# Agent attention with a feed-forward product on one core: units 2 and 3 take half of their second products in seven products per block, batches 2 and 3 get their maxima through DRAM, and the opening runs in another order

## The chip, the core and the metric

The kernel runs on one core of a Trainium2 chip. Its engines are named as in the profile: PE (TensorE, matmuls), PEld (the loading of weights into PE), DVE (VectorE), ACT (ScalarE), POOL (GpSimd) and SP (SyncE, which issues most transfers). The metric is the device time of one execution in microseconds (us). Time before: median 655.76 us of 3 runs (655.13 to 657.58).

## The reference

Eight batches of agent attention with 8 heads, 576 tokens, head size 64 and 32 memories. The tokens (4608 x 512) then go through w_in (512 x 2048), h - tanh(h), and w_out (2048 x 512):

```python
def _attn_ref(q, k, v, phi):
    a = np.exp(phi - np.max(phi, axis=2, keepdims=True))
    a = a / (np.sum(a, axis=2, keepdims=True) + 1e-09)
    k_m = np.einsum('bhsm,bhsd->bhmd', a, k)
    v_m = np.einsum('bhsm,bhsd->bhmd', a, v)
    scores = (1.0 / np.sqrt(q.shape[-1])) * np.matmul(q, k_m.transpose(0, 1, 3, 2))
    attn = np.exp(scores - np.max(scores, axis=-1, keepdims=True))
    attn = attn / (np.sum(attn, axis=-1, keepdims=True) + 1e-09)
    return np.matmul(attn, v_m)
...
h = x @ w_in
g = h - np.tanh(h)
return g @ w_out
```

## The kernel before

**Precision and products.** Large products run in fp16 pairs (high and low part), three matmuls for one. The weights arrive as 64-bit numbers, in blocks of 128 x 512 (512 KB); `conv` (words T) makes fp32 of a pair of blocks by three passes on DVE (L398, L403, L408) and the fp16 high part on ACT (L420). The low part is made in one of three ways: on DVE (`low`, Lv, L433), on ACT and POOL (`low_pool`, L, L449 and L452), or by PE and ACT (`low_pe`, Lp, L441, L442 and L444).

**Attention of a batch b.** X takes the maxima of phi over the tokens. Batches 0 and 1 use them in rows (L204, L209, then XT turns the result on PE, L218 and L220). For batches 2 and 3, XP spreads a diagonal over the partitions by an fp32 matmul (L170), and Y subtracts the result on DVE (L175, L181) ahead of the exponential on ACT. From batch 4 on, X writes the maxima to DRAM, XL loads them back to all partitions (`ms`), YM subtracts on POOL (L191, L197), and YE is the exponential. V (L238, L246) multiplies with k and v, N (L251 to L254) normalizes, U turns (L275), UV makes the fp16 pair of v (L517), S makes the scores (L290) and transposes them on DVE (L299). AM, AE, AD, AT and AS are the soft-max of a half (L318 to L338, L534); a v behind the name puts its POOL step on DVE.

**Products with the weights.** Since v_m has only 32 rows in a head, w_in is multiplied with v first: P (L543, L556) gives one of four blocks of 512 columns, PL its low part on DVE (L561), PLp the low part by PE and ACT (L568, L570).

**Units.** The tokens are cut into 18 units of 256; each has 4 blocks of 512 columns of the inner size. H (`mm1`, L591) is the first product of a unit and block; a or ap the cubic for h - tanh(h) on DVE and ACT (L606, L611, L616, L622); c or cv the low part of g on POOL or DVE (L627). M is the second product. `mm2` (L670) runs it as 24 matmuls of 512 columns. `mm2_blocks` (L727, L734), used from unit 4 on, treats the corrections as 2 x 2 blocks by seven products in place of eight: 8 matmuls of 512 columns and 28 of 256. It needs sums of blocks of g on DVE (F, `a_forms`, L640) and of w_out (G, `b_form`, L652), and collects part of its results in a PSUM tile x, which `evict` puts together at the end of a unit (L772, L773, L787 to L799). Units 0 to 3 are summed in two halves: OP saves the first half to DRAM, R loads it back, O adds the second half and writes the output (`save`, L697).

**Order.** Every engine runs its instructions in program order. Until the second block of unit 4 this order is the string START: each word starts a step, and its next occurrence runs the step's next part; words such as `i6:kv3` load blocks of weights into the buffers of the named tag, and Z is two matmuls without use (L808). Behind START a loop over the remaining blocks (slots from 18 on) runs with the plans PLAN and PLAN3.

Of the kernel before, what the change touches and what calls it, by code (L numbers as in the profile page):

```python
# [63 lines left out]
START = """
i0:gg i1:gg T00 T00 Z00 Z00 FX0 T00 X0 T00 YX0 Z00 Z00 Z00 Z00 Z00 Z00 Z00 Z00 Z00 Z00 i6:kv3 T03 i4:kv2 T03 i2:gg Z00
T02 T03 i3:gg T02 T02 Z00 KA0 Z00 Z00 Z00 KB0 Lp00 Lp00 o2:gg o3:gg Q00 T01 T03 XT0 Lp03 XT0 V00 Z00 Z00 T01 T01 T02
Q01 T01 o4:gg Lv01 o5:pp2 V01 N0 Z00 U0 L02 U0 Z00 S00 Z00 S01 T09 T09 T09 S00 o6:gg KA1 L02 KB1 AM00 S01 AM00 Lp03 UV0
UV0 o7:gg AM01 W0 T09 AM01 AE00 AE01 AD00 AD01 AD00 AT00 AD01 Z00 Z00 Z00 P00 AT01 FX1 P00 Lp09 PLp00 Z00 ASv00 P01
PLp00 ASv00 T10 Lp09 P01 AS01 H00 H00 T10 T11 PL01 i10:kv3 o9:pp4 X1 Q10 ap00 Q11 o1:gg AS01 T10 o0:pp2 T11 YX1 ap00
H10 XT1 T11 ap00 H10 XT1 T10 Lv10 ap00 c00 V10 V11 T11 L11 H11 N1 a10 U1 T08 i8:kv2 T08 UV1 U1 S10 UV1 T08 KA2 a10 T08  # L70
H11 a10 S10 H01 Lv08 a10 c10 S11 M00 ap11 AM10 W1 P10 H01 o10:pp5 o8:gg ap11 S11 ap11 M10 AM10 AE10 AM11 KB2 FA2 P10
Q20 AD10 L11 AM11 ap01 PL10 Q21 P11 T12 T12 ap01 AE11 ap11 AD10 T12 cv11 T12 P11 M11 AT10 AD11 AS10 AS10 ap01 H20 PL11
AD11 Lv12 AT11 T05 T05 ap01 T05 H21 OP1 cv01 H20 FX2 T05 ap20 H21 AS11 ap20 o11:gg AS11 X2 ap20 M01 a21 H31 L05 OP0 T04
T04 T04 a21 ap20 cv20 XP2 a21 H31 ap31 Y2 T04 L05 i14:kv3 L04 a21 L04 H30 c21 H30 a30 T13 M20 Y2 P02 i12:kv2 M21 T13
ap31 a30 P02 T13 V20 V21 a30 PL02 ap31 H02 H12 T06 T06 T06 T13 L13 OP2 T06 P12 a30 Lv06 ap31 T07 T07 N2 T07 cv30 T07 W2
M30 Lv07 P12 o12:kv2 cv31 H02 PL12 a02 P03 H12 P03 a02 T14 T14 T14 PL03 M31 ap12 a02 FA3 T14 OP3 L13 U2 ap12 Lv14 U2
UV2 o14:kv3 UV2 a02 H13 S20 ap12 S20 H13 ap12 H03 c02 AM20 a13 H03 T15 a03 P13 M02 P13 a13 S21 PL13 c12 AM20 H22 T15
a03 H23 a13 AE20 a13 G00 c13 S21 P20 AMv21 H22 AD20 a22 T15 T15 AD20 a03 a03 a22 G01 Lv15 AT20 P20 H23 a22 AMv21 AE21
cv03 ap23 R1 a22 ASv20 PL20 M12 ap23 M13 P21 ap23 FQ3 H32 ap23 P21 H32 ASv20 O1 O1 AD21 PL21 a32 H40 H40 G10 ap40 c22
R0 AD21 cv23 G20 AT21 ap40 a32 G11 ap40 H41 M03 H33 P22 AS21 H33 a32 a32 M22 P22 c32 O0 M23 X3 G21 H41 ap41 G30 ap33  # L80
G31 PL22 ap41 O0 ap33 ap40 KR30 R2 P23 P23 O2 ap41 c40 AS21 O2 ap33 ap33 F40 cv33 ap41 M32 M33 R3 O3 O3 PL23 c41
"""
# [273 lines left out]
def split_path(ctx, tc, c, ins, out):  # L356
    nc = tc.nc
# [332 lines left out]
    def save(u):  # L690

        sc = 1.0 / (S_G * S_W)
        ots = acc["r", u] if u in parts else [big.tile([P, DM], F32, tag="pr", name=f"ot{u}{tt}") for tt in range(2)]
        for tt in range(2):
            o = acc[u][tt]
            if u in parts:
                nc.vector.scalar_tensor_tensor(ots[tt], o, sc, ots[tt], op0=ALU.mult, op1=ALU.add)  # L697
            else:
                nc.scalar.activation(ots[tt], o, AF.Copy, scale=sc)
# [4 lines left out]

    def mm2_blocks(u, fb, first, last):
# [72 lines left out]
        acc["evict"] = (u, ra, rb)

    def evict():  # L780
        if "evict" not in acc:
# [5 lines left out]
        nc.vector.scalar_tensor_tensor(ra[:, 0], x[:, 1, lo], sc, ra[:, 1], op0=ALU.mult, op1=ALU.add)  # L787
        nc.vector.scalar_tensor_tensor(rb[:, 0], x[:, 1, hi], sc, ra[:, 0], op0=ALU.mult, op1=ALU.add)
        nc.vector.tensor_tensor(ra[:, 2], ra[:, 0], rb[:, 2], op=ALU.add)
        for th, r in ((0, ra[:, 1:3]), (1, rb[:, 0:2])):  # L790
            if th == (u == NUNIT - 1):
                nc.vector.tensor_tensor(rb[:, 1], rb[:, 0], rb[:, 2], op=ALU.add)
            r = r.rearrange("p a x -> p (a x)")
# [379 lines left out]
```

## Time and profile before

| | us |
|---|---|
| median of 3 runs | 655.76 |
| profiled execution | 655.77 |
| its span | 654.0 |
| PE busy | 639.2 (98%) |
| DVE busy | 518.8 (79%) |
| ACT busy | 375.0 (57%) |
| POOL busy | 251.4 (38%) |

The span is the time from the first to the last instruction of the profile; 1.77 us of the execution lie around it. Busy time of an engine is a sum over stages with different limits. PE's ends are modelled, so the durations of neighbouring matmuls overlap and the distance of their starts is the better price. A single late piece in the opening is seen better in the order of its instructions than in the shares.

### The profile page before, as it was taken

The numbers are of one execution on the slowest core, as the hardware profiler recorded it, in microseconds if no ns is written. First come the engines' busy times: TensorE is split into PE (matmuls) and PEld (weight loads), VectorE is DVE, ScalarE is ACT, GpSimd is POOL, SyncE is SP. The second block draws the span as 40 slices with busy tenths as digits, with TensorE's granted clock in tenths as the row PEclk, the third lists the DMA queues.
The fourth block names the chain that finished last, engine by engine and source line by source line (L and its number), as shares of the span: only waits on it lengthen the run. The fifth ranks groups of instructions, "written<-read, shape, count | busy, mean of one in ns | idle before, by whom it ended". The sixth has DMA issues, their size and how long they took to land.

```text
span 654.0 us, 15595 instructions
## 1 busy us (share of the span) xinstructions
PE 639.2 (98%) x6682; PEld 455.3 (70%) x6682; DVE 518.8 (79%) x786; ACT 375.0 (57%) x505; POOL 251.4 (38%) x173
## 2 busy tenths in 40 slices
PE   8889999999999999999999999999999999999996
PEld 4355656556557768777777677877687777887885
DVE  5889999999956687876897779777978686867773
ACT  3577686666524456554655566546655577666541
POOL 0225241232132154452536353624453455455531
PEclk9899999999999999999999999999999999999999
DMA  8999354402423302144323512532354333234201
GB/s 341 362 383 386 101 193 157 126 20 66 146 97 103 134 33 74 36 152 170 99 47 148 169 45 95 155 134 70 107 154 135 101 107 121 62 111 138 81 34 37
DMA packets 27724, 85.51 MB, mean 131 GB/s; under 512 B 3584, under 2 KB 4096, under 8 KB 26880
## 3 DMA queue, kind: packets, MB, share of 16 engines
q1 hardware_dynamic: 26352, 82.08, 36.9%
q10 hardware_dynamic: 1296, 2.36, 1.0%
q8 instruction: 54, 0.88, 0.5%
q14 instruction: 22, 0.18, 0.1%
HBM read 72.89 MB, written 11.54 MB: 129 GB/s over the span
## 4 chain that ended last, share of the span: by engine, by line
PE 72%; DVE 15%; issue 4%; DMA 4%; ACT 3%; POOL 2%; DVEq 0%; ACTq 0%; POOLq 0%
PE hs L591 18%; PE x L734 12%; PE o L727 12%; PE o L734 9%; PE o L670 6%; PE h L591 4%; DMA raw<-in_w_out_dram 3%; PE o1h L670 3%; DVE f L640 3%; PE pp L543 3%; DVE h L616 2%; DVE h L606 2%; DVE ph L561 2%; PE warm L808 2%; DVE wt L403 1%
## 5 line engine op out<-in xcount | busy, mean ns | idle before, releaser
L627 POOL TENSOR_TENSOR g<-h,g 128x1024 f16<-128x1024 f32 x64 | 138.6, 2166 | 322.2 <-ACT g L622 228.9
L591 PEld LDWEIGHTS <-ph 128*128 128x128 f16 x2304 | 176.9, 98 | 20.1 <-issue 6.0
L591 PE MATMUL hs<-ah,ph 128*128 128x256 f16 (+3 forms) x1152 | 151.5, 246 | 0.0
L606 DVE SCALAR_TENSOR_TENSOR h<-hs,u 128x1024 f32<-128x1024 f32 x54 | 65.8, 1219 | 90.3 <-ACT u L598 90.3
L622 ACT ACTIVATE g<-h 128x1024 f16<-128x1024 f32 x72 | 75.9, 1055 | 93.9 <-DVE h L616 91.9
L591 PE MATMUL hs<-al,ph 128*128 128x256 f16 (+3 forms) x576 | 127.6, 246 | 0.0
L611 ACT ACTIVATE u<-u,beta 128x1024 f32<-128x1024 f32 x72 | 82.4, 1147 | 52.8 <-DVE h L606 51.7
L727 PE MATMUL o<-wout_hi,g 128*128 128x512 f16 x432 | 104.7, 379 | 0.0
L734 PEld LDWEIGHTS <-f 128*128 128x128 f16 x896 | 87.7, 98 | 10.1
L616 DVE SCALAR_TENSOR_TENSOR h<-u,h 128x1024 f32<-128x1024 f32 x72 | 87.4, 1216 | 0.8 <-ACT u L611 0.7
L598 ACT ACTIVATE u<-hs 128x1024 f32<-128x1024 f32 x54 | 55.1, 1020 | 49.2 <-PE hs L591 44.9
L734 PE MATMUL x<-bt,f 128*128 128x256 f16 x672 | 82.5, 273 | 0.0
L734 PEld LDWEIGHTS <-g 128*128 128x128 f16 x672 | 64.4, 98 | 25.8 <-issue 4.3
L727 PEld LDWEIGHTS <-g 128*128 128x128 f16 x432 | 40.5, 98 | 43.9 <-issue 8.1
L640 DVE TENSOR_TENSOR f<-g 128x512 f16<-128x512 f16 x112 | 67.6, 643 | 4.3 <-POOL g L627 3.4
L670 PEld LDWEIGHTS <-g 128*128 128x128 f16 x384 | 36.7, 98 | 46.6 <-issue 3.4
L670 PE MATMUL o<-wout_hi,g 128*128 128x512 f16 x192 | 58.8, 379 | 0.0
L591 PE MATMUL h<-ah,ph 128*128 128x256 f16 (+3 forms) x384 | 49.6, 246 | 0.1
L591 PE MATMUL h<-al,ph 128*128 128x256 f16 (+2 forms) x192 | 42.4, 246 | 0.2 <-POOL al L534 0.2
L561 DVE SCALAR_TENSOR_TENSOR ph<-pp,ph 128x1024 f16<-128x1024 f32 x31 | 37.6, 1215 | 1.4 <-ACT ph L556 1.4
L556 ACT ACTIVATE ph<-pp 128x1024 f16<-128x1024 f32 x32 | 32.6, 1018 | 7.9 <-PE pp L543 5.4
L670 PE MATMUL o<-wout_lo,g 128*128 128x512 f16 x96 | 36.4, 379 | 0.0
(145 smaller groups left out, 967.0 us busy)
## 6 DMA issues: line engine op xcount, KB each, us to landing
q<-in_qt_dram SPq DMA_DIRECT2D x16, 576.0 KB, 4.7
kv<-in_kva_dram SPq DMA_DIRECT2D x16, 516.0 KB, 6.9
chk<-in_w_in_dram SPq DMA_DIRECT2D x16, 512.0 KB, 5.4
chk<-in_w_out_dram SPq DMA_DIRECT2D x16, 512.0 KB, 3.4
out_dram<-r SPq DMA_DIRECT2D x27, 256.0 KB, 2.2
kv<-in_kva_dram SPq DMA_DIRECT2D x6, 1032.0 KB, 9.0
raws<-in_w_in_dram SPq DMA_DIRECT2D x12, 512.0 KB, 7.3
raw<-in_w_out_dram SPq DMA_DIRECT2D x12, 512.0 KB, 6.4
```

Of the source, the lines that this page charges most:

```text
L561: nc.vector.scalar_tensor_tensor(pl, pa, S_P / (S_V * S_W), ph, op0=ALU.mult, op1=ALU.subtract)
L591: nc.tensor.matmul(hp[:, k, tu : tu + w], px[:, g, cs], d[ax][:, g, ta : ta + w], start=(n == 0), stop=(n == 5),)
L598: nc.scalar.activation(uu, hp, AF.Square, scale=1.0 / (S_A * S_P))
L606: nc.vector.scalar_tensor_tensor(h3, hp, C2 * S_G / (S_A * S_P), uu, op0=ALU.mult, op1=ALU.mult)
L611: nc.scalar.activation(uu, uu, AF.Square, bias=c["beta"])
L616: nc.vector.scalar_tensor_tensor(h3, uu, CC, hp, op0=ALU.add, op1=ALU.mult)
L622: nc.scalar.activation(gg[:, 0], h3, AF.Copy)
L627: eng.tensor_tensor(gg[:, 1], h3, gg[:, 0], op=ALU.subtract)
L640: nc.vector.tensor_tensor(o, x, y, op=op)
L670: nc.tensor.matmul(o, gx[:, k, P * tt : P * tt + P], wx[:, 4 * fb + k, :], start=(first and k == 0 and wx is wout_hi and gx is gh), stop=( ...
L727: nc.tensor.matmul(o[th], gg[:, 0, k, P * th : P * th + P], wout_hi[:, 4 * fb + k, :], start=(first and k == 0), stop=False)
L734: nc.tensor.matmul(dst, a(1 - n, kk), b(n, kk), start=(new and kk == 0 and n == 0), stop=(end and kk == 1 and n == 1))
```

## The change

The second products M22, M23, M32 and M33 (units 2 and 3, blocks 2 and 3) go through `mm2_blocks`, with words F22, F23, F32 and F33 for their sums of g. The assembly of `evict` is split into `sums` (four sums on DVE) and the rest; `save_blocks` puts units 2 and 3 together: the sums, two additions of o on DVE, then one addition per half on POOL of the first half that came back from DRAM. Both PSUM buffers of the first products are taken for x and hs by the word XA inside START, in place of slot 18. Batches 2 and 3 go through DRAM as the later ones do. START is written anew: block pairs of w_in are loaded and converted in another order, Lp02 and PLp01 move work from DVE to PE and ACT, four lows of weights go from DVE to ACT and POOL and two the other way, two lows of g go from DVE to POOL, and three half soft-maxes use another engine. The number of words Z is the same, 26.

```diff
-        if b > 3 and self.dram:
+        if b > 1 and self.dram:
...
+        acc["r", u] = [big.tile([P, DM], F32, tag="pr" if u < 2 else "ot", name=f"pr{u}{i}") for i in range(2)]
...
+    def sums(u):
+        ra, rb = acc.pop(("evict", u))
+        x, sc = acc["x"], 1.0 / (S_G * S_W)
+        nc.vector.scalar_tensor_tensor(ra[:, 0], x[:, 1, 0:256], sc, ra[:, 1], op0=ALU.mult, op1=ALU.add)
+        nc.vector.scalar_tensor_tensor(rb[:, 0], x[:, 1, 256:512], sc, ra[:, 0], op0=ALU.mult, op1=ALU.add)
+        nc.vector.tensor_tensor(ra[:, 2], ra[:, 0], rb[:, 2], op=ALU.add)
+        nc.vector.tensor_tensor(rb[:, 1], rb[:, 0], rb[:, 2], op=ALU.add)
+        return [r.rearrange("p a x -> p (a x)") for r in (ra[:, 1:3], rb[:, 0:2])]
+
+    def save_blocks(u):
+        rs = sums(u)
+        for r, o in zip(rs, acc[u]):
+            nc.vector.scalar_tensor_tensor(r, o, 1.0 / (S_G * S_W), r, op0=ALU.mult, op1=ALU.add)
+        yield
+        for th, (r, p) in enumerate(zip(rs, acc["r", u])):
+            nc.gpsimd.tensor_tensor(p, p, r, op=ALU.add)
+            nc.sync.dma_start(out[u * UT + P * th : u * UT + P * th + P, :], p)
+
+    def open_x():
+        acc["x"] = ps_h.tile([P, 2, 512], F32, tag="h", name="x")
+        acc["hp"] = ps_h.tile([P, 4, UT], F32, tag="h", name="hs")
...
-        "M": lambda u, fb: mm2(u, fb, fb in (0, 2), fb in (1, 3)), "R": load_part, "OP": save_part, "O": save,
+        "M": lambda u, fb: mm2_blocks(u, fb, fb == 2, fb == 3) if u in (2, 3) and fb > 1 else mm2(u, fb, fb in (0, 2), fb in (1, 3)),
+        "R": load_part, "OP": save_part, "O": lambda u: save_blocks(u) if u > 1 else save(u), "XA": open_x,
...
-        (-6, "XP{0} Y{0} | V{0}0 KR{0}1 QT{0}0"), (-5, "| V{0}1 N{0}"), (-4, "U{0} UV{0} ; W{0} | S{0}0 QT{0}1"),
+        (-6, "YE{0} | V{0}0 KR{0}1 QT{0}0"), (-5, "| V{0}1 N{0}"), (-4, "U{0} UV{0} ; W{0} | S{0}0 QT{0}1"),
...
 START = """
-i0:gg i1:gg T00 T00 Z00 Z00 FX0 T00 X0 T00 YX0 Z00 Z00 Z00 Z00 Z00 Z00 Z00 Z00 Z00 Z00 i6:kv3 T03 i4:kv2 T03 i2:gg Z00
+Z00 i6:kv3 Z00 Z00 Z00 Z00 T03 Z00 T03 T03 Z00 FX0 T03 X0 i4:kv2 i0:pp2 T02 i2:gg i3:gg i1:gg T02 T02 YX0 T01 T01 Z00
```

Three places of the new order follow, as the instructions stand on an engine: a line of the source, the operation, what is written and read (the number is that of the tile). Lines of the changed kernel stand one higher up to the second products. First SP in the opening, from the second load of q to the maxima of batch 1 (`pt`, in_phx). Before:

```order
L139 DMA q_253<-in_qt_dram 128x1152
L385 DMA raw_257<-in_w_out_dram 128x512
L385 DMA raw_261<-in_w_out_dram 128x512
L385 DMA raw_335<-in_w_out_dram 128x512
L113 DMA kv_337<-in_kva_dram 128x2064
L121 DMA kt_339<-in_kvt_dram 128x516
L113 DMA kv_343<-in_kva_dram 128x2064
L385 DMA raw_354<-in_w_out_dram 128x512
L104 DMA pt_411<-in_phx_dram 128x1152
```

Changed:

```order
L140 DMA q_317<-in_qt_dram 128x1152
L114 DMA kv_346<-in_kva_dram 128x2064
L122 DMA kt_348<-in_kvt_dram 128x516
L393 DMA raws_350<-in_w_in_dram 128x512 x2
L386 DMA raw_353<-in_w_out_dram 128x512
L386 DMA raw_437<-in_w_out_dram 128x512
L386 DMA raw_439<-in_w_out_dram 128x512
L386 DMA raw_468<-in_w_out_dram 128x512
L386 DMA raw_519<-in_w_out_dram 128x512
L105 DMA pt_525<-in_phx_dram 128x1152
```

A pair of blocks of w_in and one more block of w_out have come ahead of `pt`, and one load of k and v has gone behind it.

Second DVE, on the way from the norm of batch 1 (`kvn`) to the transpose of its first scores (`sc`); `h` is the cubic, `wt` a block of weights in the making, `vl` the low part of v. Before:

```order
L254 TENSOR_TENSOR kvn_670<-pkv_597,kr_667 128x256
L606 SCALAR_TENSOR_TENSOR h_672<-h_544,u_585 128x1024
L398 TENSOR_SCALAR wt_679<-raw_537 128x512
L398 TENSOR_SCALAR wt_680<-raw_532 128x512
L403 SCALAR_TENSOR_TENSOR wt_679<-raw_537,wt_679 128x512
L403 SCALAR_TENSOR_TENSOR wt_680<-raw_532,wt_680 128x512
L517 SCALAR_TENSOR_TENSOR vl_689<-ptr_674,vh_688 128x128
L408 SCALAR_TENSOR_TENSOR wt_679<-raw_537,wt_679 128x512
L408 SCALAR_TENSOR_TENSOR wt_680<-raw_532,wt_680 128x512
L616 SCALAR_TENSOR_TENSOR h_672<-u_585,h_672 128x1024
L299 STREAM_TRANSPOSE sc_702<-psc_693 128x576
```

Changed:

```order
L255 TENSOR_TENSOR kvn_716<-pkv_619,kr_713 128x256
L617 SCALAR_TENSOR_TENSOR h_680<-u_587,h_680 128x1024
L617 SCALAR_TENSOR_TENSOR h_684<-u_614,h_684 128x1024
L399 TENSOR_SCALAR wt_784<-raw_666 128x512
L399 TENSOR_SCALAR wt_785<-raw_596 128x512
L518 SCALAR_TENSOR_TENSOR vl_727<-ptr_718,vh_726 128x128
L404 SCALAR_TENSOR_TENSOR wt_784<-raw_666,wt_784 128x512
L404 SCALAR_TENSOR_TENSOR wt_785<-raw_596,wt_785 128x512
L409 SCALAR_TENSOR_TENSOR wt_784<-raw_666,wt_784 128x512
L409 SCALAR_TENSOR_TENSOR wt_785<-raw_596,wt_785 128x512
L300 STREAM_TRANSPOSE sc_772<-psc_763 128x576
```

The cubics of two units stand together on both sides of the norm, and the conversion of one pair of blocks still lies between the norm and the transpose.

Third DVE at the end of START, where the sums of unit 0 are saved; `f` are the new forms, `pr` the half sums and `hs` the buffer of the first product. Before:

```order
L616 SCALAR_TENSOR_TENSOR h_2126<-u_2108,h_2059 128x1024
L616 SCALAR_TENSOR_TENSOR h_2057<-u_2045,h_2057 128x1024
L697 SCALAR_TENSOR_TENSOR pr_2114<-o_1719,pr_2114 128x512
L697 SCALAR_TENSOR_TENSOR pr_2115<-o_1720,pr_2115 128x512
L151 TENSOR_REDUCE mx_2312<-pt_2014 128x2
L157 TENSOR_TENSOR dg_2314<-ident,mx_2312 128x256
L652 TENSOR_TENSOR bt_2120<-wout_lo 128x2048
L606 SCALAR_TENSOR_TENSOR h_2128<-h_2128,u_2317 128x1024
```

Changed:

```order
L697 SCALAR_TENSOR_TENSOR pr_2142<-o_1808,pr_2142 128x512
L697 SCALAR_TENSOR_TENSOR pr_2143<-o_1809,pr_2143 128x512
L617 SCALAR_TENSOR_TENSOR h_2152<-u_2146,h_2039 128x1024
L641 TENSOR_TENSOR f_2155<-g_1967 128x2x256 x2
L641 TENSOR_TENSOR f_2155<-f_2155,g_1967 128x2x256
L641 TENSOR_TENSOR f_2155<-g_1967,f_2155 128x2x256
L607 SCALAR_TENSOR_TENSOR hs<-hs,u_2211 128x1024
L641 TENSOR_TENSOR f_2239<-g_2027 128x2x256 x2
L641 TENSOR_TENSOR f_2239<-f_2239,g_2027 128x2x256
L641 TENSOR_TENSOR f_2239<-g_2027,f_2239 128x2x256
```

Where the maxima and the sums of w_out stood, the forms of f22 and f23 now stand; the maxima and the sums of w_out come earlier.

More of the change, by code (lines that the diff above doesn't have):

```diff
@@ L64 @@
 START = """
-i0:gg i1:gg T00 T00 Z00 Z00 FX0 T00 X0 T00 YX0 Z00 Z00 Z00 Z00 Z00 Z00 Z00 Z00 Z00 Z00 i6:kv3 T03 i4:kv2 T03 i2:gg Z00
[L66 to L79, printed above, removed]
@@ L80 @@
-R0 AD21 cv23 G20 AT21 ap40 a32 G11 ap40 H41 M03 H33 P22 AS21 H33 a32 a32 M22 P22 c32 O0 M23 X3 G21 H41 ap41 G30 ap33
-G31 PL22 ap41 O0 ap33 ap40 KR30 R2 P23 P23 O2 ap41 c40 AS21 O2 ap33 ap33 F40 cv33 ap41 M32 M33 R3 O3 O3 PL23 c41
+Z00 i6:kv3 Z00 Z00 Z00 Z00 T03 Z00 T03 T03 Z00 FX0 T03 X0 i4:kv2 i0:pp2 T02 i2:gg i3:gg i1:gg T02 T02 YX0 T01 T01 Z00
+Z00 Z00 T01 Z00 Z00 T00 Lp03 T00 Z00 KA0 Z00 XT0 Lp03 T00 T02 XT0 T01 KB0 Lp02 Z00 Z00 Z00 Z00 Z00 Z00 V00 Z00 L01
+o2:gg Lp02 o3:pp4 Z00 V01 T00 N0 T09 Q00 T09 L01 Lp00 U0 T09 W0 Q01 U0 UV0 S00 S01 Lp00 UV0 S00 KA1 i10:kv3 o1:gg P01
@@ new lines @@
+AM00 AM00 Z00 S01 T09 Z00 Z00 AM01 Z00 P01 AE00 PLp01 AM01 AD00 AE01 AD00 AD01 AD01 o5:pp4 o4:pp2 P00 AT00 o6:gg PLp01
+AT01 ASv00 ASv00 Lp09 P00 PLp00 PLp00 Lp09 T10 T10 T10 o7:gg T11 FX1 AS01 H00 Q11 AS01 o0:pp4 H10 X1 T10 H00 YX1 KB1
+i8:kv2 o9:pp4 XT1 T11 Lv10 H10 XT1 V10 V11 T08 T08 o8:gg Q10 T08 T08 T11 L08 o11:pp5 a00 L08 a10 H11 a00 a10 N1 U1 a00
+a00 UV1 U1 KB2 W1 H01 a10 S10 S11 H11 T12 UV1 T12 T12 a10 S10 AM10 ap11 T12 T11 L12 c10 c00 M00 H01 P10 AM10 ap11 S11
+AM11 ap01 L11 AE10 AM11 ap11 FA2 AD10 AE11 KA2 L12 Q20 ADv11 o10:gg P10 ap11 PL10 M10 ap01 AD10 Q21 i14:kv3 AT10 P11
@@ new lines @@
+ap01 cv11 T05 T05 FX2 i12:kv2 T05 L11 M11 P11 ASv10 ASv10 T05 L05 ap01 ADv11 AT11 OP1 PL11 H20 T04 cv01 L05 AS11 H20
+ap20 ap20 H21 T04 T04 T04 Lv04 ap20 AS11 T13 M01 H21 OP0 H30 a21 T13 a21 H31 T13 H30 T13 ap20 a21 H31 Lv13 ap31 P02
+ap30 P02 c20 T06 ap31 ap31 a21 c21 M20 X2 ap30 M21 ap30 PL02 ap31 c31 ap30 XL2 P12 o12:kv2 YM2 T06 T06 T06 Lv06 T07 T07
+T07 H02 H12 cv30 OP2 P12 H02 T07 Lv07 M30 PL12 H12 ap12 a02 P03 M31 T14 T14 T14 P03 PL03 a02 o14:kv3 a02 T14 YE2 ap12
+a02 V20 Lv14 T15 V21 ap12 N2 H13 OP3 T15 T15 U2 G00 H03 H22 ap12 H13 T15 a13 UV2 W2 a13 U2 G01 UV2 c02 H03 P13 cv12 a13
@@ new lines @@
+ap03 G20 G10 L15 P13 a13 PL13 ap03 H22 M02 S20 c13 H23 ap03 a22 L15 ap03 S20 AM20 a22 a22 S21 AM20 S21 AM21 AM21 R1 H23
+G21 FA3 c03 FQ3 AE20 AD20 M12 X3 a22 ap23 ap23 M13 AE21 AD20 G11 H32 ap23 AT20 ap23 O1 G30 H32 R2 H33 KR30 P20 XL3 G31
+AS20 ap32 O1 M03 ap32 c22 AD21 ap32 P20 PL20 XA AS20 R0 H33 ap33 ap33 O0 ap33 AD21 F22 ap32 H40 c23 H40 P21 ap40 F23 O0
+ap40 cv32 P21 ap33 ap40 AT21 PL21 F32 c33 M22 M23 H41 F33 O2 ap40 H41 P22 ap41 ap41 O2 P22 M32 ap41 ap41 PL22 c40 M33
+F40 O3 P23 P23 YM3 R3 PL23 cv41 O3 ASv21 ASv21
@@ L675, in load_part @@
     def load_part(u):
-        acc["r", u] = [big.tile([P, DM], F32, tag="pr", name=f"pr{u}{i}") for i in range(2)]
+        acc["r", u] = [big.tile([P, DM], F32, tag="pr" if u < 2 else "ot", name=f"pr{u}{i}") for i in range(2)]
         for r, p in zip(acc["r", u], parts[u]):
@@ L692, in save @@
         sc = 1.0 / (S_G * S_W)
-        ots = acc["r", u] if u in parts else [big.tile([P, DM], F32, tag="pr", name=f"ot{u}{tt}") for tt in range(2)]
+        ots = acc["r", u]
         for tt in range(2):
             o = acc[u][tt]
[L696 to L699, printed above, removed]
+            nc.vector.scalar_tensor_tensor(ots[tt], o, sc, ots[tt], op0=ALU.mult, op1=ALU.add)
         yield
@@ L777, in mm2_blocks @@
                 prod(*m, end=m is ms[-1])
-        acc["evict"] = (u, ra, rb)
+        acc["evict", u] = (ra, rb)
+    def sums(u):
[17 more added lines that the diff above has]
+        acc["hp"] = ps_h.tile([P, 4, UT], F32, tag="h", name="hs")
     def evict():
-        if "evict" not in acc:
+        u = next((k[1] for k in acc if isinstance(k, tuple) and k[0] == "evict"), None)
+        if u is None:
             return
-        u, ra, rb = acc.pop("evict")
-        x, o, t0 = acc["x"], acc[u], u * UT
+        o, t0 = acc[u], u * UT
         sc = 1.0 / (S_G * S_W)
         lo, hi = slice(0, 256), slice(256, 512)
[L787 to L793, printed above, removed]
+        for th, r in enumerate(sums(u)):
             if u == NUNIT - 1 and th == 1:
@@ L915, in split_path @@
     for sl, (u, fb) in enumerate(slots, 18):
-        if sl == 18:
-            acc["x"] = ps_h.tile([P, 2, 512], F32, tag="h", name="x")
-            acc["hp"] = ps_h.tile([P, 4, UT], F32, tag="h", name="hs")
         todo = ["", "", ""]
```

## The prediction

> **What bounds the kernel now.** I read the windows first, because one average over the span mixes stages with different limits. A row gives the stretch, its length, then for each engine busy microseconds and instructions, then the granted clock, the share of DMA time and GB/s.
>
> ```profile
> core 0: us, PE busy (x) PEld busy (x) DVE busy (x) ACT busy (x) POOL busy (x), PEclk, DMA share, GB/s
> ...
> 20.00:40.00 20.00, 16.54 (x205) 7.01 (x203) 16.53 (x33) 11.94 (x21) 7.34 (x7) 0.91 0.97 363
> 40.00:60.00 20.00, 16.89 (x224) 12.58 (x223) 19.17 (x29) 15.65 (x26) 4.45 (x3) 1.00 1.00 379
> 60.00:180.00 120.00, 119.94 (x1144) 70.80 (x1142) 115.98 (x152) 77.33 (x99) 33.65 (x24) 1.00 0.37 128
> 180.00:200.00 20.00, 20.00 (x160) 11.40 (x158) 11.96 (x18) 4.53 (x6) 5.51 (x3) 1.00 0.23 79
> 200.00:640.00 440.00, 438.79 (x4784) 337.27 (x4783) 337.41 (x521) 255.98 (x342) 197.36 (x127) 1.00 0.33 105
> ```
>
> From 60 us PE is full to the end. The waits of PE from 60 to 640 us say the same: one line, 1.0 us in all.
>
> ```profile
> PE pp L543 <- DVE kvn L254: 1.0, 3, 0.4
> ```
>
> So the time is the moment at which PE becomes full (the first second product, M00, at 59.0) plus all the work that PE has from there. Two things move the end: an earlier or later M00, and less or more PE work behind it. A third can appear: DVE is busy 115.98 of 120 us from 60 to 180, so it follows PE with 4 us to spare, and if it falls behind, PE waits again.
>
> **Fewer columns in the second products.** Three steps of the chain that ended last price them: one block of the plain scheme, and the two parts of a block in the seven-product scheme (start, us, engine, what, line, count).
>
> ```profile
> 162.74 5.18 PE o L670 x24
> ...
> 604.64 1.73 PE o L727 x8
> ...
> 607.24 1.75 PE x L734 x16
> ```
>
> A plain block has 24 matmuls of 512 columns, 5.18 us (0.216 each). A block in the other scheme has 8 of these (1.73) and 28 of 256 columns, at 1.75 / 16 = 0.109 each 3.06: together 4.79. Blocks M22, M23, M32 and M33 change over: 4 x (5.18 - 4.79) = **-1.56**. All of it counts, since PE never waits there; it counts for nothing only if a new wait stands behind these blocks.
>
> **Maxima through DRAM.** Batches 2 and 3 lose the fp32 matmul of the diagonal (L170).
>
> ```profile
> 89.47 0.60 PE L170 MATMUL pmx<-dg,ones 128*128 128x256 f32 x2
> 89.90 0.27 PE L591 MATMUL h<-ah,ph 128*128 128x256 f16 x1
> ```
>
> The two rows start 0.43 apart, so the pair costs PE 0.43; twice, **-0.86**. What replaces it runs elsewhere: two transfers and a subtraction on POOL.
>
> ```profile
> mxd<-mx SPq DMA_DIRECT2D x4, 1.0 KB, 3.0
> ms<-mxd SPq DMA_DIRECT2D x4, 128.0 KB, 5.3
> L191 POOL TENSOR_TENSOR e<-e,ms 128x1024 f32<-128x1024 f32 x4 | 9.6, 2400 | 0.0
> ```
>
> 3.0 + 5.3 + 2.4, the two tail rows (1.2 together, half of L191 for less than a quarter of its elements) and the exponential at about 1.2 make some 13 us. In the new order X2 stands behind M20, and V20, the first matmul that needs the result, behind M31. Between them PE has M21, M30 and M31 (3 x 5.18 = 15.5) and two first products of 24 matmuls of 256 columns (2 x 2.6), 20.7. I take the way through DRAM as hidden, with some 8 us to spare, so at 0; if ms waits behind larger loads by more than that, PE stands at V20 and each further us is lost.
>
> **The opening.** Until M00 the transfers are busy 97 to 100% of the time, and PE has waits. The piece that sets M00 begins with X1, the maxima of batch 1, for which pt1 must land. Rows of SP, of DVE and of PE:
>
> ```profile
> 10.46 10.67 SPq L385 DMA_DIRECT2D raw<-in_w_out_dram  x2
> ...
> 36.32 0.33 SPq L104 DMA_DIRECT2D pt<-in_phx_dram  x1
> ```
>
> ```profile
> 42.36 1.33 DVE L204 TENSOR_REDUCE mx<-pt 128x2 f32<-128x1152 f32 x1
> 43.62 1.22 DVE L606 SCALAR_TENSOR_TENSOR h<-h,u 128x1024 f32<-128x1024 f32 x1
> 44.75 1.28 DVE L408 SCALAR_TENSOR_TENSOR wt<-raw,wt 128x512 uint32<-128x512 uint32 x2
> ...
> 48.35 1.21 DVE L616 SCALAR_TENSOR_TENSOR h<-u,h 128x1024 f32<-128x1024 f32 x1
> 49.49 1.28 DVE L433 SCALAR_TENSOR_TENSOR wout_lo<-wt,wout_hi 128x512 f16<-128x512 f32 x2
> 50.69 0.15 DVE L251 TENSOR_SCALAR kr<-pkv 128x2 f32<-128x2 f32 x1
> ...
> 51.41 1.22 DVE L606 SCALAR_TENSOR_TENSOR h<-h,u 128x1024 f32<-128x1024 f32 x1
> 52.76 0.76 DVE L398 TENSOR_SCALAR wt<-raw 128x512 uint32<-128x512 uint32 x2
> 53.44 1.28 DVE L403 SCALAR_TENSOR_TENSOR wt<-raw,wt 128x512 uint32<-128x512 uint32 x2
> 54.64 0.28 DVE L517 SCALAR_TENSOR_TENSOR vl<-ptr,vh 128x128 f16<-128x128 f32 x1
> 54.84 1.28 DVE L408 SCALAR_TENSOR_TENSOR wt<-raw,wt 128x512 uint32<-128x512 uint32 x2
> ...
> 57.17 0.78 DVE L299 STREAM_TRANSPOSE sc<-psc 128x576 f32<-128x576 f32 x1
> ```
>
> ```profile
> 58.36 0.71 PE L290 MATMUL psc<-q,kT 64*32 64x288 f32 x16
> 59.00 0.39 PE L670 MATMUL o<-wout_hi,g 128*128 128x512 f16 x1
> ```
>
> SP stood 10.67 us at one load of w_out that had no free buffer, and issued pt1 at 36.32; X1 ran 42.36 to 43.62. In the new order the loads up to and with pt1 are 17 blocks of weights of 512 KB, four of 576 KB (q and phi), three of 1032 KB and two of 258 KB (k and v; sizes from the shapes): 14,620 KB, 14.97 MB. At the 379 GB/s of the window they take 39.5 us, from 0.74 us on: pt1 lands at about 40.2, and X1 ends at 41.5, **2.1 earlier** than before. This holds if SP stands nowhere long, since the loads fill a queue; it is the weakest term.
>
> Behind X1 DVE then has, up to the transpose of S10 (starts one apart in the rows above): pairs of weight passes, 2 x 0.68 (L398) and 6 x 1.20 (L403, L408); one pair of L433, 1.20; two each of L606 (1.13) and L616 (1.14), 4.54; the norm, 0.72; vl, 0.20. That is 15.2. Before, the same stretch was 13.55 (43.62 to 57.17). So the transpose starts at 41.5 + 15.2 + 0.2 (the waits that were in it before) = 56.9, ends 0.7 later, S11 follows at once in the new order and takes 0.64 (58.36 to 59.00): M00 at 58.25, **-0.75**. Bounds: the whole 2.1 if DVE's rows fit into its waits as they move, and nothing if a load comes late.
>
> PE gets two more pieces ahead of M00: Lp02 (two fp32 matmuls of 512 columns and two fp16 ones) and PLp01, the three passes of a product again.
>
> ```profile
> 31.55 0.41 PE L543 MATMUL pp<-win_hi,vh 64*32 64x512 f16 x8
> ...
> 32.32 1.13 PE L441 MATMUL pw<-wt,idw 128*128 128x512 f32 x2
> 33.28 0.38 PE L442 MATMUL pw<-wout_hi,nid 128*128 128x512 f16 x1
> ```
>
> At most 2 x (1.13 + 0.38) and 3 x 0.41 with two of 0.38: 5 us at the outside. PE has 6.6 us without work from 20 to 60, so I cost them at nothing; half of that cover is ahead of X1, and without it 1 or 2 us of the lead would go.
>
> **The end of the opening, DVE and POOL.** Prices of what they gain and lose (busy, mean ns):
>
> ```profile
> L640 DVE TENSOR_TENSOR f<-g 128x512 f16<-128x512 f16 x112 | 67.6, 643 | 4.3 <-POOL g L627 3.4
> L640 DVE TENSOR_TENSOR f<-g,f 128x512 f16<-128x512 f16 x56 | 24.8, 442 | 1.9
> L787 DVE SCALAR_TENSOR_TENSOR r<-x,r 128x256 f32<-128x256 f32 x14 | 5.9, 418 | 2.1 <-ACT r L773 2.1
> L175 DVE TENSOR_TENSOR e<-e,pmx 128x1024 f32<-128x1024 f32 x2 | 2.4, 1218 | 0.0
> ```
>
> DVE gains four times the forms (2 x 0.643 + 2 x 0.44 = 2.2), two times four sums (4 x 0.42 = 1.7), and one soft-max row more (of the transpose's size, 0.8): 12.9. It loses two of L175 with diagonal and tails (2 x 2.4, the small ones taken as one more of its size), two lows of g (its size, 2 x 1.2), four of L433 (4 x 0.6) and one PL (1.2): 10.8. So **DVE has about 2 us more in all**, but the losses lie early and the gains late, before the third block of unit 4 at some 200 us. There the window 180:200 has DVE at 11.96 of 20: 8 us free, for a surplus of some 10 behind an early relief that gives it about as much lead. I cost it at 0. POOL gains two maxima with their tails (2 x 3.6), four additions (half of L191 each, 4.8), and two lows of g at 2.4 or less: some 17 us, where it was busy 33.65 of 120.
>
> [...] The row L640 f<-g has a mean of 643 ns, and the trace has single ones much longer:
>
> ```profile
> L640 DVE TENSOR_TENSOR f<-g x112: 382/419/1968, 184.7 to 643.1; 128x512 f16<-128x512 f16 x112
> ```
>
> [...]
>
> **Sum.** Against the profiled run of 655.77 (span 654.0), which stands 0.01 over the median of 655.76: -0.75 - 1.56 - 0.86 = -3.17, so **652.6**.
>
> **Rivals.**
> 1. The whole lead of X1 reaches M00 (2.1 in place of 0.75): 651.2. For it: every wait of PE in the opening hangs on DVE or ACT. Against: DVE has 1.65 us more to do behind X1.
> 2. The lead is lost, because a weight block comes late: T10 and T08 need blocks that wait for buffers of the products: 653.4, or 653.9 with half a us more.
> 3. PE has longer pauses in the opening and gets a slower clock. The window 20:40 has 0.91 granted, which costs 0.09 x 20 = 1.8. One more such stretch: 652.6 + 1.8 = 654.4. The order of the warm-up matmuls changes, their number doesn't, so I hold this for small. [...]
> 4. Slower: the forms at the end of the opening become the bound. Where POOL is at work, each of the two f<-g of a block takes 1.97 in place of 0.42, four blocks 4 x 2 x 1.55 = 12.4; less the some 5 us that DVE is ahead, PE waits 7.4: 660.0. It decides from the point at which DVE has less than 12 us of lead and free time at M22. Against: 8 free us in 180:200 and the early relief; POOL is not busy all the time.
> 5. The change does less than it says: the matmuls of 256 columns cost as much as those of 512, 112 x 0.107 = +12, 664.6. The chain's row of 16 in 1.75 excludes it nearly.
>
> **How the numbers follow.** A measurement of this kernel can tell some 0.5%, 3.3 us, from no change: faster is under 652.5, slower over 659.0. The forecast has 0.50, rival 1 0.15, rival 2 0.16, rival 3 0.09, rival 4 0.08, rival 5 0.02. The forecast lies just at the bound, so a little under half of it counts as faster: with rival 1, 0.38; slower is rivals 4 and 5, less the part of 4 that stays under 659: 0.08; the rest, 0.54, is no change. The range goes from 650.0 (rival 1 and 1.2 us of the 1.8 that the slow clock costs today) to 657.0 (rival 3 with half of the 5 us that the extra PE work could cost): 0.85 of the cases.
>
> **What would show it.** In the profile after: M00 at about 58.2, X1 ending at 41.5; no wait of PE over 1 us in sum from 60 to 200; the four blocks with 28 matmuls at 0.109 each; V20 and V30 without a wait on the exponential; forms of f22 to f33 with a mean under 0.8. It is wrong if X1 is not earlier than 43, if PE waits at M22 to M33 for f, or if the clock in the first 60 us is under 0.9 in more than one window.

## The result and the profile after

The changed kernel takes 658.99 us (median of 22 runs, 655.24 to 671.86) against 655.45 before (22 runs, 654.78 to 657.92): ratio 1.0054 (1.0041 to 1.0066). It is about 0.5% slower, where 652.6 was forecast. The run of 671.86 fell in a slower state of the chip (clock 0.949) and is not in the ratio. The profiled run took 658.27 (span 656.5, M00 at 60.21). The windows of the changed kernel, in the columns of before:

```profile
core 0: us, PE busy (x) PEld busy (x) DVE busy (x) ACT busy (x) POOL busy (x), PEclk, DMA share, GB/s
...
20.00:40.00 20.00, 16.13 (x238) 6.59 (x227) 14.24 (x30) 10.29 (x19) 7.46 (x6) 1.00 1.00 391
40.00:60.00 20.00, 17.06 (x234) 13.73 (x234) 19.71 (x34) 17.32 (x30) 5.39 (x4) 1.00 0.96 353
60.00:180.00 120.00, 116.49 (x1105) 70.14 (x1093) 114.51 (x147) 76.44 (x98) 50.80 (x31) 1.00 0.39 131
180.00:200.00 20.00, 20.00 (x245) 15.43 (x243) 18.19 (x30) 8.71 (x11) 10.66 (x9) 1.00 0.22 72
```

PE was full from 60 to 180 before (119.94) and is not now (116.49), while POOL went from 33.65 to 50.80. The waits of PE from 60 to 200 (total, times, longest):

```profile
PE psc L291 <- DVE ph L562: 1.5, 1, 1.5
PE pkv L239 <- ACT e L201: 0.9, 1, 0.9
PE h L592 <- DVE h L607: 0.7, 1, 0.7
PE h L592 <- DVE h L617: 0.4, 1, 0.4
```

That makes 3.5 us, all between 122 and 144, where before had none. M00 is 1.2 later, and behind it, with the waits taken off, 2.2 less is left (before: 654.0 - 59.0 - 1.0 of waits = 594.0; after: 656.5 - 60.2 - 4.5 = 591.8). So the profiled run comes out: 655.8 + 1.2 + 3.5 - 2.2 = 658.3. The 2.2 is what is left over in this sum, not a measurement of its own. The median is another 0.7 higher; that part is put down to the clock below, but no run isolates it.

The 1.2 is also that of one profile. Four kernels of the experiments have the same order up to M00 and, like this profile, no stretch of lower clock ahead of it: their M00 came at 59.62 to 59.91, so the new opening costs 0.6 to 1.2 against the 59.0 of before.

Where DVE is late ahead of two of these waits (those at 123 and 142), its rows and POOL's tell why. Which memory a row reads is taken from the tile's pool in kernel.py: PSUM where the pool says so, as for the products of PE, else SBUF. POOL, then DVE, at the subtraction of batch 2's maxima:

```profile
108.35 2.97 POOL L192 TENSOR_TENSOR e<-e,ms 128x1024 f32<-128x1024 f32 x1 [5.86 <-DMA ms<-mxd]
...
107.18 1.29 DVE L404 SCALAR_TENSOR_TENSOR wt<-raws,wt 128x512 uint32<-128x512 uint32 x2
108.39 3.49 DVE L409 SCALAR_TENSOR_TENSOR wt<-raws,wt 128x512 uint32<-128x512 uint32 x2
```

The second L409 row (from 108.99, 2.89 in place of 0.68) ended at 111.88, 0.56 after POOL's row. From there DVE ran late, and ACT behind it: the exponential for the wait at 123 stood behind a conversion that waited for DVE.

```profile
120.65 1.23 ACT L421 ACTIVATE wout_hi<-wt 128x512 f16<-128x512 f32 x2 [1.27 <-DVE wt L409]
121.79 1.15 ACT L201 ACTIVATE e<-e 128x1152 f32<-128x1152 f32 x1
```

And at a sum of w_out (G10):

```profile
137.78 2.42 POOL L628 TENSOR_TENSOR g<-h,g 128x1024 f16<-128x1024 f32 x1 [10.41 <-ACT g L623]
...
136.98 1.22 DVE L653 TENSOR_TENSOR bt<-wout_hi 128x2048 f16<-128x2048 f16 x1
138.12 3.16 DVE L653 TENSOR_TENSOR bt<-wout_hi,bt 128x2048 f16<-128x2048 f16 x1
141.20 1.21 DVE L562 SCALAR_TENSOR_TENSOR ph<-pp,ph 128x1024 f16<-128x1024 f32 x1
142.33 1.21 DVE L617 SCALAR_TENSOR_TENSOR h<-u,h 128x1024 f32<-128x1024 f32 x1
```

The sum of 1.2 us began after POOL's row, stood until that ended at 140.20, and ended 1.08 later. The two rows behind it read PSUM; beside POOL's next row (L453, from 140.15 on) they take their usual 1.21. In this profile DVE loses time beside POOL only in rows that read nothing but SBUF, such as these two (2.89 in place of 0.68, 3.16 in place of 1.22), and only to a POOL row that began first. Not every such row loses time; the last section says which. An estimate, from each stretched row against the usual length of the same row: from 60 to 200 DVE stood behind POOL for 8.9 us, where it was 3.0 in before. Before lost 2.0 of these between 125 and 145 without a wait of PE, so the loss alone does not make a wait: it has to fall ahead of a row that PE needs soon.

### The profile page after: what moved, and what is told of

The parts are those of the page before. It is cut to its first block, busy times and chain, and to the rows that moved or that the text cites. A ratio compares the mean times of both kernels' runs of the same rounds, so it can differ in the third digit from the quotient of the medians.

```text
span 656.5 us, 15803 instructions
## 1 busy us (share of the span) xinstructions
PE 638.0 (97%) x6758; PEld 460.7 (70%) x6758; DVE 523.8 (80%) x796; ACT 380.3 (58%) x513; POOL 275.9 (42%) x186
## 4 chain that ended last, share of the span: by engine, by line
PE 68%; DVE 18%; issue 6%; POOL 3%; DMA 2%; ACT 2%; ACTq 0%; SPq 0%; DVEq 0%; POOLq 0%
PE hs L592 19%; PE x L732 13%; PE o L725 13%; PE o L732 10%; PE o1h L671 3%; DVE f L641 3%; DVE h L617 3%; PE pp L544 3%; DVE h L607 2%; DVE wt L404 2%; DVE wt L409 2%; POOL g L628 2%; PE o L671 2%; DVE ph L562 2%; PE warm L825 1%
## 5 line engine op out<-in xcount | busy, mean ns | idle before, releaser
L628 POOL TENSOR_TENSOR g<-h,g 128x1024 f16<-128x1024 f32 x66 | 144.4, 2190 | 290.8 <-ACT g L623 186.1
L592 PE MATMUL hs<-ah,ph 128*128 128x256 f16 (+3 forms) x1216 | 157.2, 245 | 0.0
L592 PE MATMUL hs<-al,ph 128*128 128x256 f16 (+3 forms) x608 | 133.1, 245 | 0.0
L725 PE MATMUL o<-wout_hi,g 128*128 128x512 f16 x464 | 112.6, 379 | 0.0
L732 PEld LDWEIGHTS <-f 128*128 128x128 f16 x960 | 93.9, 98 | 10.9
L732 PE MATMUL x<-bt,f 128*128 128x256 f16 x720 | 88.4, 273 | 0.0
L641 DVE TENSOR_TENSOR f<-g 128x512 f16<-128x512 f16 x120 | 72.6, 645 | 4.3 <-POOL g L628 3.4
L592 PE MATMUL h<-ah,ph 128*128 128x256 f16 (+2 forms) x320 | 44.1, 251 | 2.1 <-ACT ph L571 0.9
L671 PE MATMUL o<-wout_hi,g 128*128 128x512 f16 x128 | 39.3, 379 | 0.0
L592 PE MATMUL h<-al,ph 128*128 128x256 f16 (+2 forms) x160 | 37.0, 251 | 0.2 <-POOL al L535 0.2
L732 PE MATMUL o<-bt,g 128*128 128x256 f16 x240 | 36.0, 273 | 0.0
```

Of the source, the lines that this page charges most:

```text
L592: nc.tensor.matmul(hp[:, k, tu : tu + w], px[:, g, cs], d[ax][:, g, ta : ta + w], start=(n == 0), stop=(n == 5),)
L628: eng.tensor_tensor(gg[:, 1], h3, gg[:, 0], op=ALU.subtract)
L641: nc.vector.tensor_tensor(o, x, y, op=op)
L671: nc.tensor.matmul(o, gx[:, k, P * tt : P * tt + P], wx[:, 4 * fb + k, :], start=(first and k == 0 and wx is wout_hi and gx is gh), stop=( ...
L725: nc.tensor.matmul(o[th], gg[:, 0, k, P * th : P * th + P], wout_hi[:, 4 * fb + k, :], start=(first and k == 0), stop=False)
L732: nc.tensor.matmul(dst, a(1 - n, kk), b(n, kk), start=(new and kk == 0 and n == 0), stop=(end and kk == 1 and n == 1))
```

## The experiments

Each run is compared with before on its own chip: before was 655.95 in the first set, 656.04, 655.25, 655.78 and 655.76 in the others. Lines in the profiles shift by one to three with the edits.

**pt1 in a free buffer.**

```diff
-"FX": lambda b: att.load_phx(b, st[b]),
+"FX": lambda b: att.load_phx(b, st[b], "qt" if b == 1 else "sc"),
```

> The changed kernel, but phi of batch 1 (pt1) is loaded into the q buffer of the later batches, which is free in the opening, in place of the ring of two score buffers. Ring theory: in the changed kernel pt1 was issued only at 37.36, when the transpose AT01 let go of a score buffer (37.3), so X1 ran 42.04 to 43.31; with a free buffer SP issues pt1 by about 32, X1 starts at 40.0 to 40.5, and M00 comes 1.5 to 2 us before the 60.21 of the changed kernel, time 1 to 2 us less. Rival (the transfers themselves are late): X1 starts no earlier than 41.5 and M00 stays within 0.4 of 60.21.

Measured: ratio 1.0056 (1.0040 to 1.0072), M00 at 59.76. In the changed kernel SP issued pt1 at 37.36, as the buffer came free, and X1 (L205) began at 42.04. With the free buffer (SP, then DVE):

```profile
31.47 0.33 SPq L105 DMA_DIRECT2D pt<-in_phx_dram  x1
...
40.96 0.75 DVE L399 TENSOR_SCALAR wt<-raw 128x512 uint32<-128x512 uint32 x2
41.76 1.35 DVE L205 TENSOR_REDUCE mx<-pt 128x2 f32<-128x1152 f32 x1
```

Issued 5.9 earlier, pt1 landed 10.3 after its issue, at about the time when DVE had done the rows ahead of X1 (T10 and T11, without a pause from 37.85). The ring theory falls; two limits meet at 41.6. M00 is no earlier than in the kernels below that leave this load alone (59.62 to 59.91).

**Maxima of batches 2 and 3 subtracted on DVE.**

```diff
-m, e, eng = ..., d["e"], self.tc.nc.gpsimd
+m, e, eng = ..., d["e"], self.tc.nc.vector if b in (2, 3) else self.tc.nc.gpsimd
 START: YM2 moved behind cv30
```

> The changed kernel, but the subtraction of the maxima of batches 2 and 3 (from the copy loaded from DRAM) runs on DVE, after cv30, in place of POOL. Port theory: POOL's subtraction stretched DVE's rows beside it (the L409 pair at 108.39 took 3.49 in place of 1.28, two more rows 0.26 each, 2.7 in all), more than the 1.8 that DVE needs to do it itself; the pair is back at 1.3, PE's waits from 60 to 200 fall from 3.5 to 2.5 or less, time 0.5 to 1.5 less. Rival (DVE is simply too full, and stretch plays no part): 1.8 us more on DVE, PE's waits rise to 4 to 5, time 0.5 to 1.5 more.

What the expectations call the port theory is tested here by what it says of the times: that DVE's rows are stretched beside POOL's (3.49 in place of 1.28) and that PE's waits come from it. No run shows what holds the rows. Measured: 1.0031 (1.0018 to 1.0043), 0.23% under the changed kernel; the two intervals just touch. DVE has 1.8 us more to do and is done sooner:

```profile
109.03 1.28 DVE L411 SCALAR_TENSOR_TENSOR wt<-raws,wt 128x512 uint32<-128x512 uint32 x2
110.23 1.21 DVE L630 TENSOR_TENSOR g<-h,g 128x1024 f16<-128x1024 f32 x1
111.37 1.21 DVE L194 TENSOR_TENSOR e<-e,ms 128x1024 f32<-128x1024 f32 x1
```

Behind M00 the wait of 0.9 for the exponential is gone, the others (2.6) stay. The theory expected 2.5 or less, so it holds to 0.1.

**Plain blocks for units 2 and 3.**

```diff
-"M": lambda u, fb: mm2_blocks(u, fb, fb == 2, fb == 3) if u in (2, 3) and fb > 1 else mm2(...),
+"M": lambda u, fb: mm2(u, fb, fb in (0, 2), fb in (1, 3)),
 START: without F22 F23 F32 F33; R3 ahead of M32; the old save
```

> The changed kernel with the plain 24-matmul blocks for M22, M23, M32 and M33, without the forms F22 to F33 and with the old save of units 2 and 3; everything else as changed. If the block change was priced right and is fully kept: PE has 1.56 us more work, the waits from 120 to 145 stay as they are, time 1.3 to 1.9 more than the changed kernel. If forms and POOL at the end of the opening give the gain back (the fourth rival of the prediction): within 0.5 of the changed kernel or faster.

Measured: 1.0059 (1.0045 to 1.0074); the same four waits. From M00 to the end of the span it has 657.5 - 59.64 = 597.9, the changed kernel 656.5 - 60.21 = 596.3: the blocks are worth 1.6 and keep all of it. Over all runs the ratio is only 0.05% above the changed kernel's, less than the expected 1.3 to 1.9 us. All six runs here had a clock of 0.998 or more, which only 11 of the 21 runs in the changed kernel's ratio had; between runs of that clock the median span differs by 1.4 (657.5 against 656.1).

**The old opening with the new rest**, two kernels: START of before up to M00, then the words of the changed kernel that are left; in the second with the sums moved (next run) and T12 behind cv11.

> The order of before up to M00, then the order of the changed kernel for all that is left (blocks in seven products, maxima of batches 2 and 3 through DRAM). Two separate losses (opening 1.2, waits 3.5): M00 at 59.0 as before, the waits from 60 to 200 still 2.5 to 4.5, time about 656 to 657.5. If the waits only come from the late opening: they fall under 1, time about 653 to 654.

> The order of before up to M00, with T12 and L12 behind cv11 as there, then the order of the second run of this set. If the loss of 1.2 at M00 lies in the new opening alone: M00 at 59.0 to 59.4, PE's waits from 60 to 200 as in the second run, time 0.8 to 1.5 less than it, 654 to 655. Rival (the new opening takes work off DVE that the rest then needs): M00 as said, but waits from 60 to 200 over 1.5 and time no better than the second run.

Measured: 1.0140 (1.0119 to 1.0162) and 1.0217 (1.0194 to 1.0240). M00 came at 59.37 and 58.57, so the new opening does cost about 1. But new waits stand behind it (5.3 at 76 in the first, 8.2 between 71 and 85 in the second), in part perhaps from where T12 was put, which was not tried apart. The first missed its expected times by over 6 us; in the second the rival held. Neither gives a price for the opening alone; they show that the rest needs what the new opening does earlier.

**Sums of w_out moved**, alone, with the subtraction on DVE, and with that and three words Z more:

```diff
-U2 G00 H03 ... U2 G01 UV2 c02 ... G20 G10 L15 P13 a13 PL13
+U2 H03 ... U2 UV2 G00 G01 c02 ... G20 L15 P13 a13 PL13 G10
 third kernel: Z00 Z00 ahead of S00, Z00 ahead of S01
```

> The changed kernel; three sums of w_out on DVE are only moved: G00 behind the second part of UV2, with G01 behind it, and G10 behind PL13, where POOL is idle. No work is added or taken away. Port theory: the row bt<-wout_hi,bt, which took 3.16 at 138.12 and ended 1.08 after POOL's low of g, takes 1.2; PE's waits of 0.65 at 132 and of 1.52 and 0.41 at 142 to 144 go, waits from 60 to 200 fall from 3.5 to 1.3 or less, time 1.8 to 2.6 less than the changed kernel. Rival (DVE is too full): the waits come back at the next place, sum still 2.8 or more, time within 0.7 of the changed kernel.

> The sums moved as in the run before, and the subtraction of the maxima of batches 2 and 3 on DVE. Port theory: both waits are gone, PE's waits from 60 to 200 are 0.6 or less, time 2.7 to 3.5 less than the changed kernel, 655.0 to 656.2. Rival (DVE is too full): the 1.8 us more on DVE bring a wait of 1 or more before 145, time above 656.5.

> The run before with three words Z more (six matmuls without use): two ahead of S00 and one ahead of S01, where PE waits 1.2 and 0.7 for q. Clock theory: the single runs of the changed kernel fall in steps with the granted clock (0.998 to 1.0 gives 655.2 to 658.5, 0.996 gives 659.5 to 659.8, 0.991 to 0.994 gives 660.4 to 664.4), since PE's pauses from 25 to 35 bring half-rate windows into the path to M00; with the pauses filled nearly all runs have 0.998 or more, the runs lie within 1.5 of each other and the median is 0.6 to 1.5 under that of the run before. Rival (the pauses are not the cause): clock and spread as in the run before, median 0 to 0.9 higher, by the matmuls added.

Measured: 1.0064 (1.0045 to 1.0083), 1.0037 (1.0016 to 1.0058) and 1.0030 (1.0015 to 1.0044). By these numbers the rivals held in all three. But the places were bad ones: G10 now stood ahead of a row of the cubic that frees PSUM. The waits of the second, 60 to 200, and its windows there:

```profile
PE h L594 <- DVE h L619: 2.4, 1, 2.4
PE psc L293 <- DVE ph L564: 0.6, 1, 0.6
```

```profile
140.00:142.00 2.00, 0.14 (x8) 0.10 (x1) 2.00 (x2) 0.00 (x0) 2.00 (x2) 1.00 0.30 48
142.00:144.00 2.00, 1.50 (x19) 1.45 (x19) 2.00 (x3) 1.44 (x2) 1.45 (x2) 0.66 0.61 247
144.00:146.00 2.00, 2.00 (x21) 1.91 (x19) 1.97 (x3) 0.76 (x1) 0.87 (x1) 0.50 0.00 0
146.00:148.00 2.00, 2.00 (x34) 1.13 (x33) 0.47 (x2) 1.00 (x2) 1.21 (x1) 0.99 0.03 8
```

After a wait of 2.4 the clock is at half for 1.4 + 2.0 = 3.4 us, which costs 1.7 more. The added Z hardly changed the single runs' clocks (0.993 to 0.998 without, 0.995 to 0.998 with), so the pauses before 35 us are not the main cause there.

**Sums moved again**, with the subtraction on DVE. G00 and G01 directly ahead of UV2's second part; G10 ahead of G11; then, in a second kernel, both of these behind the last part of ap23.

```diff
-AE21 AD20 G11 H32 ap23 AT20 ap23 O1
+AE21 AD20 G10 G11 H32 ap23 AT20 ap23 O1
 second kernel:
+AE21 AD20 H32 ap23 AT20 ap23 G10 G11 O1
```

> The changed kernel with the subtraction of the maxima of batches 2 and 3 on DVE, G00 and G01 directly ahead of the second part of UV2 (DVE stood 1.5 there in the last such run) and G10 directly ahead of G11, some 15 us later than in the changed kernel. The theory now: PE's waits between 120 and 145 come from DVE's rows that read only SBUF standing behind a POOL instruction, and from rows of w_out's sums put ahead of rows that free PSUM; each wait of over 2 us also brings a stretch of about 3.4 us at half clock, 1.7 more. With both out of the way: waits from 60 to 200 of 0.5 or less, no granted clock under 0.99 after 60 us in the profile, time 654.3 to 655.6 and runs within 1.5 of each other. Rival (DVE is too full in 120 to 160, wherever the rows stand): waits of 1.5 or more, time 657 or more.

> The run e_fix2 with G10 and G11 behind the last part of ap23 (the cubic's second pass, whose lateness was the one wait of 1.90 at 155). Port theory: that wait goes, because POOL's low of g no longer stands ahead of G11 with the cubic behind it; waits from 60 to 200 of 0.6 or less, no half clock after 60, time 653.8 to 654.8, a little under before. Rival (DVE too full): a wait of 1 or more further on, time 655.5 or more.

Measured: 1.0016 (1.0007 to 1.0025) and **0.9979 (0.9967 to 0.9991)**: 654.47, 0.2% faster than before, and 0.75% under the changed kernel by the two ratios. The waits of the first and of the second (its psc row is S11, ahead of M00 at 60.77):

```profile
PE h L594 <- DVE h L619: 1.9, 1, 1.9
```

```profile
PE psc L293 <- DVE sc L302: 1.2, 1, 1.2
PE h L594 <- DVE pr L699: 0.2, 1, 0.2
```

The first missed its number by one more wait: G11 began 1.0 after a POOL row, a low of g, had begun and took 3.15. With it out of the way 120 to 200 is clean, as expected, with no work taken from DVE: by the same estimate as above DVE stands behind POOL for 2.8 from 60 to 200, where it was 8.9. That DVE has too much work of its own is thereby ruled out as the cause. DVE's stand behind POOL, and the place of the sums ahead of rows that free PSUM, are not told apart: the move took the sums away from both at once.

**The blocks on the old order.** START of before up to M13, then the changed order, batch 2 by the diagonal.

> The order of before up to M13 (its opening, batch 2 by the matmul of the diagonal), then the order of the changed kernel: M22, M23, M32 and M33 in seven products, batch 3 through DRAM, the sums of w_out that are still missing spread over that stretch. Theory: the blocks are worth 4 x 0.39 = 1.56 and one matmul pair 0.43, and the loss lies in the new opening and in 120 to 145; M00 at 59.0, time 653.6 to 654.6. Rival (the fourth of the prediction: forms and sums at the end of the opening are too much for DVE, which had 10 us free from 150 to 200 and gets some 10 more): waits of 1.5 to 5 between 160 and 205 and time 656 to 660.

Measured: 1.0174 (1.0156 to 1.0192). M00 at 58.88, but 8.4 us of waits between 155 and 180:

```profile
PE x L734 <- DVE h L619: 4.8, 1, 4.8
PE h L594 <- DVE h L619: 2.1, 1, 2.1
PE hs L594 <- DVE al L537: 1.6, 1, 1.6
```

Ahead of the 4.8 DVE itself stood 4.32 for a half sum from DRAM (`pr<-d`), so this order is bad for that reason as well. What it does show is that the blocks cannot just be put into the old order at that point.

**The opening.** T12 behind S11's transpose and H01 between S10 and S11; then the load Q10 ahead of i8, with and without that.

```diff
-H01 a10 S10 S11 H11 T12 UV1 T12 T12 a10 S10 AM10 ap11 T12 ... S11 AM11
+a10 S10 H01 S11 H11 UV1 a10 S10 AM10 ap11 ... S11 T12 T12 T12 AM11 T12
 the two others: Q10 behind KB1
```

> The run above, and in the opening the conversion T12, which the blocks of M02 need only at about 150, is moved from ahead of the transpose of S10 to behind that of S11, and H01 stands between S10 and S11, so that PE has work while DVE transposes. Theory: M00 hangs on DVE's rows ahead of the transpose (15.4 from X1 on, of them 3.1 of T12); the 1.54 that PE stood before S11 goes, M00 at 58.6 to 59.0, time 0.5 to 1.3 less than the run above. Rival (the rows are only put off and DVE has no free time behind): M00 as said, but waits of 1 or more between 60 and 120, time the same or more than the run above.

> The run e_open, with the load of q for S10 (word Q10) moved ahead of the loads i8 and o9, so that SP issues it at 42 to 43 in place of 48.9. In e_open PE stood 2.51 for this load and a stretch at half clock followed. Theory (three limits at nearly one time: this load at 56.7, PE's own work, and DVE's rows at 58.1): with the load early S10 starts at 54.5 to 55.5, no half clock at 56 to 60, M00 at 58.6 to 59.2, time 653.4 to 654.4. Rival (T12 put off costs as much behind M00): M00 as said, waits from 60 to 120 of 1.2 or more, time 655 or more.

> The run e_fix3 with only the load Q10 moved as in the run before; T12 and H01 stay. If DVE's rows set M00 there, the load has no part in it: S10's transpose within 0.5 of 58.7, M00 at 59.6 to 60.8, time within 0.6 of e_fix3. If the load set it: M00 0.8 or more earlier and time as much less.

Measured: 1.0051 (1.0031 to 1.0071), 1.0056 (1.0043 to 1.0069) and 1.0035 (1.0011 to 1.0059). The first stood 2.5 for q, with 3.4 us at half clock from there on, and M00 came at 62.22 in place of the expected 58.6 to 59.0. In the second S10's transpose began at 56.32, 2.4 before the changed kernel's 58.73, and M00 at 59.45, but T12 now ran beside POOL, whose rows held it, and PE waited 3.2 at 68.8 (POOL, then DVE; then that wait):

```profile
57.59 4.23 POOL L630 TENSOR_TENSOR g<-h,g 128x1024 f16<-128x1024 f32 x2 [5.47 <-ACT g L625]
...
60.33 3.07 DVE L401 TENSOR_SCALAR wt<-raw 128x512 uint32<-128x512 uint32 x2
63.32 1.28 DVE L406 SCALAR_TENSOR_TENSOR wt<-raw,wt 128x512 uint32<-128x512 uint32 x2
```

```profile
PE o1h L673 <- DVE h L619: 3.2, 1, 3.2
```

The rival held. In the third the transpose came at 58.21 and M00 at 59.69. The first kernel of "Sums moved again" has the same opening without the moved load, and 58.12 and 59.62: the load alone does not set it. (The second kernel there has M00 at 60.77, but its profile caught a stretch of half clock at 28.6 to 32.0.) The time missed its expectation by far. Its twelve runs go from 654.3 (clock 0.999) to 661.7 (0.994), where those of the kernel without the moved load lay within 654.0 to 655.4; why this one falls to the lower clock so often stays open, since its profile shows a run without it.

## Why the prediction was wrong

- **Fewer columns, -1.56: right.** The run with plain blocks measured 1.6, all of it kept. PE's work behind M00 fell by 2.2 in all, forecast 2.42; the part of the diagonals (0.86) was not tried alone.
- **The opening, -0.75: wrong, +1.2.** The failing step is X1, "2.1 earlier than before". It came 0.3 earlier (42.04, ending 43.4). The rate was not the error: 378 GB/s on average from 0.74 to 42.0. The sum had 0.6 MB less than had moved by then (14.97 against 15.59), took SP to stand nowhere long, and did not count the rows of DVE ahead of X1. pt1 stood for its buffer until 37.36, would have landed at 41.7 anyway, and DVE was not free before 41.6. The sum behind it was right: 15.2 forecast, 15.3 measured (43.4 to 58.73). M00 missed 58.25 by the 1.9 that X1 missed.
- **DVE and POOL, costed at 0: wrong, +3.5.** POOL's 17 us more were booked as work of an engine that is off the path. The fourth rival had DVE's rows longer beside POOL (1.97 in place of 0.42) but looked for them at the forms; where PE felt it, it struck at 108 and 138, where DVE converts weights and sums w_out. The forms went from a mean of 643 to 645 ns, and PE did not wait at M22 to M33. The row of 3.16 at 138.12 is POOL's rest of 2.08 (to 140.20) and 1.08 more, for a row that takes 1.22 where POOL is idle (158.79). Not all of the 3.5 is this stand alone: the sums were also put ahead of rows that free PSUM, and the run that moved them within 130 to 145 only moved the wait.
- **Maxima through DRAM, "some 8 us to spare": right, yet V20 waited.** POOL had done the subtraction at 113.60, 8.2 before the exponential began at 121.79. On ACT the exponential stood behind the conversion T14, whose last rows on DVE came late after the stop at 108; that is where the 0.9 comes from. The way through DRAM had its room; the place of the exponential in ACT's order was not part of the sum. With the subtraction on DVE, where nothing stopped at 108, this wait was gone.
- **The clock (third rival): right in part.** Single runs of the changed kernel fall in steps with their mean granted clock: 655.2 to 658.5 at 0.998 and more (11 runs), 659.5 to 659.8 at 0.996 (5), 660.4 to 664.4 at 0.991 to 0.994 (5). In the profiles that show a half-rate stretch behind M00, it came with a wait of PE. Once the waits were gone, eleven runs lay within 1.4 us of each other; but with the load Q10 moved twelve runs lay 7.4 apart, and the profile there has no wait over 0.2 behind M00, so the waits are not the only source. The windows above, behind a wait of 2.4, add up to 3.4 us at half clock. Where the stretches of the changed kernel's lower runs lie was not seen, as its profile caught a run without them. The rival's place, the opening, counts too: two profiles with the changed opening have a stretch at 28.6 to 32.2 and M00 at 60.77 and 60.83, about 1 later than those without.

The range (650.0 to 657.0) was too narrow because it added the clock to the forecast but gave the waits of DVE a place late in the opening only.
